# Plain product for the second block, rounding and block sums spread over turns, all score masks on VectorE

## The chip, the cores and the metric

The kernel runs on one core of a Trainium2 chip. The core has a matrix engine (TensorE, "PE" in the profile; its weight loads, "PEld", overlap the matmuls), a vector engine (VectorE, "DVE"), an activation engine (ScalarE, "ACT"), a general engine (GpSimd, "POOL") and a queue that issues most transfers (SyncE, "SP"). Each engine works off its own instructions in order; engines wait for each other through semaphores. The metric is the device time of one execution in microseconds: 628.98 us before the change, the median of three runs.

## The reference

Two parts follow each other: a gated linear attention (a state of 48 x 48 per head that decays and takes in one outer product per time step), and a feed-forward layer whose activation is h erf(softplus(h)).

```python
B, H, S, D = 4, 8, 768, 48
f = 1.0 / (1.0 + np.exp(-f_logit))
for t in range(S):
    state = f[:, :, t, :, None] * state + np.einsum('bhd,bhe->bhde', k[:, :, t], v[:, :, t])
    y[:, :, t] = np.einsum('bhd,bhde->bhe', q[:, :, t], state)
x = y.transpose(0, 2, 1, 3).reshape(3072, 384)
h = x @ w_in                                  # w_in 384 x 2048
sp = np.maximum(h, 0.0) + np.log1p(np.exp(-np.abs(h)))
out = (h * erf(sp)) @ w_out                   # w_out 2048 x 384
```

The two weights arrive with 64 bits a number.

## The kernel before

The 3072 tokens are 24 chunks of 128 and 12 blocks of two chunks. A chunk `g` passes four stages: `stage_d` (cumulated decays, decayed q and k), `stage_t` (transposes), `stage_s` (scores of the two half chunks, masked, and the new state) and `stage_y` (output, 128 tokens by 384). A block then gives 16 hidden tiles in four groups (`hidden`), each group is activated in ten steps (`activate`), and a projection makes the output rows.

An outer loop of 12 turns weaves all this together. One **slot** is one matmul of the hidden layer or the projection; the loop emits a slot and then, by counters, other work: a step of rounding, a stage of a chunk, a step of the activation, a step of sums. In turn `it`, the chunks of block it + 2 are worked on, the hidden tiles of block it + 1 are made, and block it - 2 is projected (from turn 2 on; turns 0 and 1 have hidden slots only).

```python
    def slots(it):

        if it == 0:
            h0, h1 = hiddens(0), hiddens(1)
            order = [h0[0], h0[1], h1[0], h0[2], h1[1], h0[3], h1[2], h1[3]]
            return chain(*order), 2 * n_h
        if it == 1:
            return chain(*hiddens(2)), n_h
        if it == 2:
            return chain(*hiddens(3), project_first(0)), n_h + n_ft * CPB
        if it < n_blocks - 1:
            return chain(project(it - 2), *hiddens(it + 1)), n_o + n_h
        return chain(*[project(blk) for blk in range(n_blocks - 3, n_blocks)]), 3 * n_o
```

**Masks.** The scores of a half chunk must keep only earlier time steps. Up to chunk 2 and from chunk 10 on VectorE multiplies them by a triangle straight from PSUM; for chunks 3 to 9 ScalarE copies and GpSimd masks:

```python
        for c in range(2):
            for r in range(2):
                if FIRST <= g < 2 * ADJACENT:

                    nc.scalar.copy(out=qA[half(1 - r), r, :, half(c)], in_=sc[half(c), r])
                    if c == 1:
                        flat = qA[half(1 - r), r].rearrange("s a (c t) -> s (a c) t", c=2)
                        nc.gpsimd.affine_select(
                            out=flat, in_=flat, pattern=[[0, 2 * HP], [1, C]], compare_op=ALU.is_ge,
                            fill=0.0, base=0, channel_multiplier=-1,
                        )
                    continue
                nc.vector.tensor_tensor(
                    out=qA[half(1 - r), r, :, half(c)], in0=sc[half(c), r],
                    in1=tri1[half(c)].unsqueeze(1).broadcast_to((C, HP, C)), op=ALU.mult,
                )
```

**Rounding.** Both weights come in 16 pieces of 768 KB (eight of `w_in`, then eight of `w_out`). `round_piece` turns one into 32 bits: one pass on ScalarE, then six on VectorE of 128 x 768 (lines 313 to 336). `weights_step` does about one of the six at a time, and the loop says how many per slot:

```python
            gen, n = slots(it)
            if it == 0:
                todo = [(stage_s, 2), (stage_y, 2), (stage_d, 3), (stage_t, 3), (stage_s, 3), (stage_y, 3),
                        (stage_d, 4), (stage_t, 4), (stage_d, 5), (stage_s, 4), (stage_t, 5),
                        (stage_y, 4)] + stages(2)[4:]
                at = [1, 5, 6, 12, 16, 23, 34, 42, 48, 52, 60, 74, 76, 80, 88, 94]
# ...
            for s, _ in enumerate(gen):
                due += (1 if s < 42 else 0.6 if s < 72 else 0.3) if it == 0 else 0.42 if it == 1 else 0.6
                while due >= 1:
                    weights_step()
                    due -= 1
```

**Projection.** Block 0 is projected plainly: 32 slots with 384 columns (`project_first`). The others use Winograd's form of Strassen's product: 7 products in place of 8, so 56 slots with 192 columns (`project`). It needs sums of blocks of the hidden (`sum_h`, four per group, on VectorE, once the group is activated), sums of blocks of `w_out` (`sum_w`, once, on GpSimd), and a combination of the products (L725).

```python
    def add(out, x, y, op=ALU.add, engine=nc.vector):
        engine.tensor_tensor(out=out, in0=x, in1=y, op=op)

    def sum_w(gi):
        w = w_out_sb[:, FG * gi : FG * (gi + 1), :]
        b11, b12 = w[:, 0:2, 0:DH], w[:, 0:2, DH:]
        b21, b22 = w[:, 2:4, 0:DH], w[:, 2:4, DH:]
        t = w_sums(gi)
        add(t[:, 0], b12, b11, ALU.subtract, nc.gpsimd)
        yield
        add(t[:, 1], b22, t[:, 0], ALU.subtract, nc.gpsimd)
        yield
        add(t[:, 2], b22, b12, ALU.subtract, nc.gpsimd)
        yield
        add(t[:, 3], b21, t[:, 1], ALU.subtract, nc.gpsimd)
# ...
    def sum_h(gr):

        while not gr["done"]:
            act_step()
        a11, a12, a21, a22 = blocks(gr["h"])
        sums = next(sum_places)
        add(sums[0], a21, a22)
        yield
        add(sums[1], sums[0], a11, ALU.subtract)
        yield
        add(sums[2], a12, sums[1], ALU.subtract)
        yield
        add(a21, a11, a21, ALU.subtract)
        gr["sums"] = sums
# ... in project_first, after the last slot of a group:
                    if j == FG - 1 and tt == CPB - 1:
                        to_sum.append(sum_w(gi))
# ... in project:
            for gi in gis:
                gr = groups[blk, gi]
                while gr["sums"] is None:
                    sum_step()
                        nc.tensor.matmul(
                            place[n], lhsT=x[:, j, :], rhs=y,
                            start=(gi == 0 and j == 0 and n in first),
                            stop=(gi == n_g - 1 and j == 1), skip_group_check=True,
                        )
                        yield
```

The sums of `w_out` are kept where the hidden of block 0 lay (`wT`), so each can be made only after block 0's product of that group.

**Activation steps and sum steps** in the loop:

```python
                if it < 2:
                    step = it == 1 and s % 6 == 3
                elif it == 2:
                    step = s % 5 in (1, 3)
                else:
                    step = s % 9 in (2, 6)
                if step:
                    act_step()
                if it == 2:
                    if s == n - 6:
                        to_sum.extend(sum_h(groups[1, gi]) for gi in range(NS))
                    sum_step()
                elif it > 2:
                    if s == n_o and it < n_blocks - 1:
                        to_sum.extend(sum_h(groups[it - 1, gi]) for gi in range(NS))
                    if it == n_blocks - 1 and s % n_o == 40 and s < 2 * n_o:
                        blk = n_blocks - 2 + s // n_o
                        to_sum.extend(sum_h(groups[blk, gi]) for gi in range(NS))
                    if s < n_o or s % 3 == 0 or it == n_blocks - 1:
                        sum_step()
```

```python
        h = gr["h"].rearrange("p j t -> p (j t)")
        e = epool.tile([P, FG * TB], FP32, name="e", tag="e")
        exp(e, h)
        yield
        n = len(SERF_KAB)
        xs = {}
        for i in range(n):
            xs[i] = xpool.tile([P, FG * TB], FP32, name="x", tag="x")
            other_set()
            term(xs[i], h, i)
            yield
        for i in range(n):
            times(e, xs[i], i)
            yield
        for _ in range(3):
            yield
        other_set()
        nc.scalar.activation(out=e[:], in_=e[:], func=AF.Tanh, scale=SERF_C)
        yield
        nc.vector.tensor_tensor(out=h, in0=h, in1=e[:], op=ALU.mult)
        gr["done"] = True
```

`act_step` moves each group that is being activated on by one step; a new group starts when the last has had five. `sum_h` calls `act_step` itself, as often as it takes, when its group is not activated yet.

Of the kernel before, what the change touches and what calls it, by code (L numbers as in the profile page):

```python
# [74 lines left out]
def kernel(  # L75
# [21 lines left out]
    CPB = 2  # L97
# [345 lines left out]
    def stage_s(g):  # L443
# [40 lines left out]
        for c in range(2):  # L484
            for r in range(2):
                if FIRST <= g < 2 * ADJACENT:

                    nc.scalar.copy(out=qA[half(1 - r), r, :, half(c)], in_=sc[half(c), r])  # L488
                    if c == 1:
                        flat = qA[half(1 - r), r].rearrange("s a (c t) -> s (a c) t", c=2)  # L490
                        nc.gpsimd.affine_select(
                            out=flat, in_=flat, pattern=[[0, 2 * HP], [1, C]], compare_op=ALU.is_ge,
                            fill=0.0, base=0, channel_multiplier=-1,
                        )
                    continue
# [105 lines left out]
    def places():  # L601
        own = [[sums_sb[:, b, n] for n in range(NA)] for b in range(NS)]
        for _ in range((n_blocks - 3) * n_g // NS):
# [4 lines left out]
        own = own[1::-1] + own[3:] + own[2:3]  # L608
# [5 lines left out]
    def add(out, x, y, op=ALU.add, engine=nc.vector):  # L614
        engine.tensor_tensor(out=out, in0=x, in1=y, op=op)  # L615

    def sum_w(gi):
# [4 lines left out]
        add(t[:, 0], b12, b11, ALU.subtract, nc.gpsimd)  # L622
        yield
        add(t[:, 1], b22, t[:, 0], ALU.subtract, nc.gpsimd)
        yield
        add(t[:, 2], b22, b12, ALU.subtract, nc.gpsimd)
        yield
        add(t[:, 3], b21, t[:, 1], ALU.subtract, nc.gpsimd)
# [30 lines left out]
    def project_first(blk):  # L659

        ops = ps_moe.tile([P, 2, 512], FP32, name="ops", tag="moe")
        for gi in range(n_g):
            gr = groups[blk, gi]
            for tt in range(CPB):
                for j in range(FG):
# [10 lines left out]
                    if j == FG - 1 and tt == CPB - 1:  # L676
                        to_sum.append(sum_w(gi))
# [82 lines left out]
    def slots(it):  # L760
# [7 lines left out]
        if it == 2:  # L768
            return chain(*hiddens(3), project_first(0)), n_h + n_ft * CPB
        if it < n_blocks - 1:  # L770
# [19 lines left out]
    with tc.manual_schedule():  # L790
# [8 lines left out]
        load(1, "qk")  # L799
        load_f(2)  # L800
        load_piece(0)
        load(1, "v")
        load(2)
        load_piece(1)
# [58 lines left out]
        stage_t(0)  # L863
        load(3, "qk")
# [327 lines left out]
```

## Time and profile before

| | before |
|---|---|
| time, median of 3 (lowest to highest) | 628.98 us (628.93 to 629.83) |
| span of the profiled execution | 627.6 us |
| TensorE busy | 589.5 us (94%), 5777 matmuls |
| VectorE busy | 470.2 us (75%), 788 instructions |
| ScalarE busy | 382.4 us (61%), 483 instructions |
| GpSimd busy | 38.4 us (6%), 49 instructions |
| mean granted TensorE clock | 0.974 |

Every matmul of 32-bit operands in the source is two matmul instructions in the trace. Busy time overlaps between the engines: it says how long an engine had work in hand, not that the work set the end. TensorE's mean durations overlap too (a matmul is in flight while the next starts), so the pace of a row of matmuls is read from the length of the row and not from the mean of one. The page's second part cuts the span into 40 slices of 15.7 us, a digit each (9 is 90% or more):

```profile
PE   8788699998976999999999999999999999999995
DVE  4998998695589778678787876797887694756751
ACT  5725457978864457756675776765775656556200
POOL 1000011010176000000000000000000000000000
PEclk9879799999989899999999999999999999999999
DMA  9997743440321043043052052052030000000000
```

The first six slices are full of transfers and of VectorE's work, GpSimd works mostly in slices 11 to 13, and from about the sixteenth slice on TensorE is full. A digit below 9 in the clock row is a slice in which TensorE ran slower for a part.

### The profile page before, as it was taken

To read this page: it belongs to the slowest core of one execution; us is meant where nothing else is said; L and a number is where in the kernel's file an instruction comes from. 1 tells how busy PE (TensorE), PEld (TensorE's weight loads), DVE (VectorE), ACT (ScalarE), POOL (GpSimd) and SP (SyncE) were. 2 spreads that over 40 slices of the span, in tenths; PEclk is the share of its full clock that TensorE was granted. 3 is DMA by queue.
4 is the path that set the end of the run, shared out by engine and by line. 5 is a ranking of instruction groups with operands and counts; after the bars stand their busy time and mean duration, and the time that the engine had idled before them with its cause. 6 is when DMAs were issued, how large, how long until landed. Compare 5 with 4: busy or idle time off the path is not lost.

```text
span 627.6 us, 13891 instructions
## 1 busy us (share of the span) xinstructions
PE 589.5 (94%) x5777; PEld 524.7 (84%) x5777; DVE 470.2 (75%) x788; ACT 382.4 (61%) x483; POOL 38.4 (6%) x49
## 2 busy tenths in 40 slices
PE   8788699998976999999999999999999999999995
PEld 7567588887644988988998998998998989989995
DVE  4998998695589778678787876797887694756751
ACT  5725457978864457756675776765775656556200
POOL 1000011010176000000000000000000000000000
PEclk9879799999989899999999999999999999999999
DMA  9997743440321043043052052052030000000000
GB/s 200 247 241 215 216 123 63 88 78 12 63 56 26 1 78 76 1 79 75 4 102 52 2 102 51 3 102 52 3 76 14 2 27 1 19 8 1 25 26 29
DMA packets 155587, 41.35 MB, mean 66 GB/s; under 512 B 147328, under 2 KB 150400, under 8 KB 155520
## 3 DMA queue, kind: packets, MB, share of 16 engines
q1 hardware_dynamic: 153440, 40.02, 29.3%
q8 instruction: 47, 0.77, 0.5%
q10 hardware_dynamic: 2080, 0.39, 0.3%
q14 instruction: 20, 0.16, 0.1%
HBM read 35.59 MB, written 4.72 MB: 64 GB/s over the span
## 4 chain that ended last, share of the span: by engine, by line
PE 72%; DVE 12%; issue 6%; ACT 5%; DMA 2%; SPq 1%; POOL 1%; DVEq 0%; ACTq 0%; POOLq 0%
PE ops L717 31%; PE hps L587 29%; PE y L525 3%; PE ps_t L411 2%; PE ops L670 2%; PE ps_d L380 2%; DVE sv L438 1%; PE sc L460 1%; PE sc L468 1%; DVE sv L439 1%; DVE w_in_sb L322 1%; DMA qn<-in_q_dram 1%; DVE qA L496 1%; DVE w_in_sb L336 1%; ACT L160 1%
## 5 line engine op out<-in xcount | busy, mean ns | idle before, releaser
L587 PE MATMUL hps<-xT,w_in_sb 128*128 128x256 f32 x1152 | 264.7, 386 | 7.8 <-DVE w_in_sb L336 4.4
L587 PEld LDWEIGHTS hps<-xT,w_in_sb 128*128 128x128 f32 x1152 | 218.2, 192 | 41.2 <-DVE w_in_sb L336 3.4
L165 DVE SCALAR_TENSOR_TENSOR e<-x,e 128x1024 f32<-128x1024 f32 x96 | 120.2, 1252 | 13.5 <-ACT x L160 13.2
L160 ACT ACTIVATE x<-Hg,serf_bias 128x1024 f32<-128x1024 f32 x88 | 97.6, 1141 | 0.2
L157 ACT ACTIVATE e<-Hg 128x1024 f32<-128x1024 f32 x44 | 46.6, 1058 | 77.0 <-DVE Hg L561 73.2
L717 PE MATMUL ops<-wT,Hg 128*128 128x192 f32 x352 | 87.6, 331 | 0.0
L717 PE MATMUL ops<-wT,scratch 128*128 128x192 f32 x320 | 76.5, 331 | 5.9 <-DVE scratch L615 5.9
L717 PE MATMUL ops<-w_out_sb,Hg 128*128 128x192 f32 x352 | 72.6, 329 | 0.0
L561 DVE TENSOR_TENSOR Hg<-Hg,e 128x1024 f32<-128x1024 f32 x44 | 54.6, 1240 | 22.5 <-ACT e L559 22.4
L717 PEld LDWEIGHTS ops<-wT,Hg 128*128 128x128 f32 x352 | 62.1, 192 | 2.2
L594 ACT COPY Hg<-hps 128x1024 f32<-128x1024 f32 x44 | 44.4, 1010 | 31.0 <-PE hps L587 30.7
L717 PEld LDWEIGHTS ops<-w_out_sb,Hg 128*128 128x128 f32 x352 | 60.7, 192 | 2.6
L717 PEld LDWEIGHTS ops<-wT,scratch 128*128 128x128 f32 x320 | 57.0, 193 | 6.2 <-issue 6.2
L559 ACT ACTIVATE e<-e 128x1024 f32<-128x1024 f32 x48 | 50.4, 1050 | 6.4 <-DVE e L165 6.3
L496 DVE TENSOR_TENSOR qA<-sc,tri 64x256 f32<-64x256 f32 x68 | 28.7, 422 | 22.3 <-PE sc L468 21.3
L725 DVE TENSOR_TENSOR scratch<-scratch,ops 128x384 f32<-128x384 f32 (+1 forms) x44 | 22.2, 504 | 30.3 <-ACT scratch L733 25.0
L418 ACT COPY qA<-ps_t 64x512 f32<-64x512 f32 x48 | 27.7, 578 | 22.5 <-PE ps_t L411 20.6
L395 DVE TENSOR_TENSOR qd<-qn,dp 128x384 f32<-128x384 f32 x24 | 13.4, 556 | 35.6 <-ACT dp L383 34.4
L717 PE MATMUL ops<-w_out_sb,scratch 128*128 128x192 f32 x160 | 39.5, 328 | 0.0
L525 PEld LDWEIGHTS y<-qA,sv 128*32 128x32 f32 x1536 | 24.6, 113 | 17.2 <-issue 9.2
L525 PE MATMUL y<-qA,sv 128*32 128x64 f32 x1536 | 28.9, 226 | 9.3 <-issue 6.9
L438 DVE TENSOR_TENSOR sv<-sc,sv 48x192 f32<-48x192 f32 x80 | 28.4, 354 | 8.3 <-ACT qA L488 6.9
(109 smaller groups left out, 648.9 us busy)
## 6 DMA issues: line engine op xcount, KB each, us to landing
lt<-in_f_logit_dram SPq DMA_DIRECT2D x24, 192.0 KB, 3.8
qn<-in_q_dram SPq DMA_DIRECT2D x24, 192.0 KB, 3.3
out_dram<-scratch SPq DMA_DIRECT2D x12, 384.0 KB, 2.6
kn<-in_k_dram SPq DMA_DIRECT2D x23, 192.0 KB, 3.5
vt<-in_v_dram SPq DMA_DIRECT2D x23, 192.0 KB, 3.6
sv<-in_v_dram SPq DMA_DIRECT2D x84, 48.0 KB, 2.9
w_out_sb<-in_moe_w_in_dram SPq DMA_DIRECT2D x4, 768.0 KB, 6.3
Hg<-in_moe_w_in_dram SPq DMA_DIRECT2D x4, 768.0 KB, 6.4
```

The lines of the kernel that those rows point to most:

```text
L157: nc.scalar.activation(out=dst[:], in_=h, func=AF.Exp)
L160: nc.scalar.activation(out=dst[:], in_=h, func=AF.Tanh, bias=serf_bias[:, i : i + 1], scale=SERF_KAB[i][0])
L165: nc.vector.scalar_tensor_tensor(out=e[:], in0=x[:], scalar=SERF_KAB[i][2], in1=e[:], op0=ALU.add, op1=ALU.mult)
L418: nc.scalar.copy(out=qAs[g][half(r), r], in_=pss[0][half(r)])
L438: nc.vector.tensor_tensor(out=new, in0=add, in1=old, op=ALU.add)
L496: nc.vector.tensor_tensor(out=qA[half(1 - r), r, :, half(c)], in0=sc[half(c), r], in1=tri1[half(c)].unsqueeze(1).broadcast_to((C, HP, C)), ...
L525: nc.tensor.matmul(y[M * i : M * (i + 1), kt, half(c)], lhsT=sv[:, r, c, a, o : o + M], rhs=qA[:, r, a, half(c)], start=(n == 0), stop=Tru ...
L559: nc.scalar.activation(out=e[:], in_=e[:], func=AF.Tanh, scale=SERF_C)
L561: nc.vector.tensor_tensor(out=h, in0=h, in1=e[:], op=ALU.mult)
L587: nc.tensor.matmul(hps[:, j, :], lhsT=w_in_sb[:, kt, ft * P : (ft + 1) * P], rhs=xTs[blk][:, kt, :], start=(kt == 0), stop=(kt == n_k - 1),)
L594: nc.scalar.copy(out=gr["h"], in_=hps[:])
L717: nc.tensor.matmul(place[n], lhsT=x[:, j, :], rhs=y, start=(gi == 0 and j == 0 and n in first), stop=(gi == n_g - 1 and j == 1), skip_grou ...
```

## The change

It alters five things together and leaves what is computed as it is.

- **Masks.** All chunks are masked on VectorE; the branch for chunks 3 to 9 goes.
- **Second block plain.** Block 1 is projected by `project_first` as block 0 is, at the start of turn 3, and needs no sums.
- **Block sums of w_out** are made by VectorE instead of GpSimd, on every second slot of turns 2 and 3.
- **Rounding** is spread: fewer steps per slot in turn 0, the last ones in turn 2.
- **Schedule.** Activation starts in turn 0 and its steps are spaced anew; the first two pieces of weights are loaded earlier and chunk 1's q and k later; the slots at which the stages of turns 0 and 3 are emitted move.

It is meant to even out VectorE's load and to take GpSimd and the early sums out of the way of the matmuls. The diff, with the plain renames and the list of places for the sums cut:

```diff
@@ stage_s
-                if FIRST <= g < 2 * ADJACENT:
-
-                    nc.scalar.copy(out=qA[half(1 - r), r, :, half(c)], in_=sc[half(c), r])
-                    if c == 1:
-                        flat = qA[half(1 - r), r].rearrange("s a (c t) -> s (a c) t", c=2)
-                        nc.gpsimd.affine_select(
-                            out=flat, in_=flat, pattern=[[0, 2 * HP], [1, C]], compare_op=ALU.is_ge,
-                            fill=0.0, base=0, channel_multiplier=-1,
-                        )
-                    continue
                 nc.vector.tensor_tensor(
@@ sum_w (and the same for the three others)
-        add(t[:, 0], b12, b11, ALU.subtract, nc.gpsimd)
+        add(t[:, 0], b12, b11, ALU.subtract)
@@ project_first
-                        to_sum.append(sum_w(gi))
+                        if blk == 0:
+                            to_sum.append(sum_w(gi))
@@ slots
+        if it == 3:
+            return chain(project_first(1), *hiddens(4)), n_ft * CPB + n_h
@@ the first loads
-        load(1, "qk")
+        load_piece(0)
+        load(1, "qkv")
+        load_piece(1)
         load_f(2)
-        load_piece(0)
-        load(1, "v")
         load(2)
-        load_piece(1)
         load_piece(2)
@@ before the first turn
         stage_t(0)
+        weights_steps(2)
         load(3, "qk")
@@ the turns
-                todo = [(stage_s, 2), (stage_y, 2), (stage_d, 3), (stage_t, 3), (stage_s, 3), (stage_y, 3),
+                todo = [(stage_s, 2), (stage_d, 3), (stage_y, 2), (stage_t, 3), (stage_s, 3), (stage_y, 3),
-                at = [1, 5, 6, 12, 16, 23, 34, 42, 48, 52, 60, 74, 76, 80, 88, 94]
+                at = [1, 5, 8, 12, 16, 23, 36, 43, 48, 52, 60, 74, 76, 80, 88, 94]
-                at = ([0] if it + 2 == ADJACENT else []) + [2, 26, 42, 54, 76, 90]
+                at = [0, 1, 15, 24, 31, 52, 66] if it + 2 == ADJACENT else [2, 26, 42, 54, 76, 90]
-                due += (1 if s < 42 else 0.6 if s < 72 else 0.3) if it == 0 else 0.42 if it == 1 else 0.6
+                due += (1 if s < 18 else 0.46 if s < 66 else 0.3) if it == 0 else 0.45
-                if it == 0 and s == 14:
+                if it == 0 and s == 24:
                     prepare(2, 0, CPB)
-                if it < 2:
-                    step = it == 1 and s % 6 == 3
-                elif it == 2:
-                    step = s % 5 in (1, 3)
+                if it == 0:
+                    step = s >= 24 and s % 8 == 5
+                elif it == 1:
+                    step = s % 5 == 3
+                elif it < 4:
+                    step = s % 7 in (1, 4)
+                elif it == n_blocks - 1:
+                    step = s % 3 == 1
                 else:
                     step = s % 9 in (2, 6)
                 if it == 2:
-                    if s == n - 6:
-                        to_sum.extend(sum_h(groups[1, gi]) for gi in range(NS))
-                    sum_step()
+                    if s % 2:
+                        sum_step()
                 elif it > 2:
-                    if s == n_o and it < n_blocks - 1:
+                    if s == n - n_h and it < n_blocks - 1:
                         to_sum.extend(sum_h(groups[it - 1, gi]) for gi in range(NS))
-                    if s < n_o or s % 3 == 0 or it == n_blocks - 1:
+                    if it == 3:
+                        if s % 2:
+                            sum_step()
+                    elif s < n_o or s % 3 == 0 or it == n_blocks - 1:
                         sum_step()
```

More of the change, by code (lines that the diff above doesn't have):

```diff
@@ L602, in places @@
         own = [[sums_sb[:, b, n] for n in range(NA)] for b in range(NS)]
-        for _ in range((n_blocks - 3) * n_g // NS):
+        for _ in range((n_blocks - 4) * n_g // NS):
             yield from own
@@ L607, in places @@
             own.insert(0, [x[:, 0 : S_WORDS // (NS * NA)].rearrange("p (j t) -> p j t", j=FG // 2) for x in t])
-        own = own[1::-1] + own[3:] + own[2:3]
+        own = own[1::-1] + own[2:]
         while True:
@@ L612, with add @@
     sum_places = places()
-    def add(out, x, y, op=ALU.add, engine=nc.vector):
-        engine.tensor_tensor(out=out, in0=x, in1=y, op=op)
+    def add(out, x, y, op=ALU.add):
+        nc.vector.tensor_tensor(out=out, in0=x, in1=y, op=op)
     def sum_w(gi):
@@ L621, in sum_w @@
         t = w_sums(gi)
-        add(t[:, 0], b12, b11, ALU.subtract, nc.gpsimd)
+        add(t[:, 0], b12, b11, ALU.subtract)
         yield
-        add(t[:, 1], b22, t[:, 0], ALU.subtract, nc.gpsimd)
+        add(t[:, 1], b22, t[:, 0], ALU.subtract)
         yield
-        add(t[:, 2], b22, b12, ALU.subtract, nc.gpsimd)
+        add(t[:, 2], b22, b12, ALU.subtract)
         yield
-        add(t[:, 3], b21, t[:, 1], ALU.subtract, nc.gpsimd)
+        add(t[:, 3], b21, t[:, 1], ALU.subtract)
     def blocks(h):
```

## The prediction

> **What bounds the kernel now.** I first read the page's busy shares (TensorE 94%, VectorE 75%, ScalarE 61%, GpSimd 6%), then the chain of work that ended last, and found where each turn of the outer loop begins by counting the matmuls of L587, L670 and L717 in TensorE's timeline. The windows of turns 0 to 3, with turn 5 as an undisturbed one, are this table (columns: TensorE, its weight loads, VectorE, ScalarE, GpSimd busy, then clock, DMA share and GB/s):
>
> ```profile
> 28.30:106.50 78.20, 67.99 (x739) 55.60 (x740) 72.72 (x120) 37.49 (x61) 5.80 (x8) 0.87 0.70 176
> 106.50:134.50 28.00, 27.59 (x368) 23.13 (x368) 20.61 (x36) 26.14 (x38) 3.15 (x4) 1.00 0.42 73
> 134.50:192.50 58.00, 52.12 (x440) 37.92 (x439) 41.59 (x49) 42.44 (x52) 19.60 (x16) 0.97 0.27 48
> 192.50:250.50 58.00, 51.03 (x535) 46.24 (x534) 47.79 (x80) 33.51 (x39) 6.81 (x7) 0.94 0.24 49
> 298.10:344.50 46.40, 46.40 (x487) 42.50 (x486) 36.93 (x65) 30.95 (x36) 0.00 (x0) 1.00 0.28 53
> ```
>
> From 298 us nearly to the end TensorE has no gap: the kernel is bound by matmuls there and only less matmul work could shorten it. What can be gained lies before. I work out the matmul time of a turn from undisturbed stretches of the chain: a hidden slot (two instructions) takes 20.72/96 x 2 = 0.432 us, a Winograd product slot 54.62/336 x 2 = 0.325 us, a plain projection slot (384 columns) twice that, 0.65 us, and one chunk of the attention (L380, L411, L460, L468, L525) 0.65 + 0.87 + 1.0 + 1.03 = 3.55 us. Turn 0 (96 hidden slots, 4 chunks) then needs 41.5 + 14.2 = 55.7 us and takes 78.2. Turn 1 (48, 2) needs 27.8 and takes 28. Turn 2 (48 hidden, 32 plain, 2 chunks) needs 20.7 + 20.8 + 7.1 = 48.6 and takes 58. Turn 3 (56 products, 48 hidden, 2 chunks and one extra score stage) needs 18.2 + 20.7 + 7.1 + 1.0 = 47 and takes 58. Turn 4 takes 47.6 against 46.4. That is 22.5 + 0.2 + 9.4 + 11 + 1.2 = 44 us above the matmul floor.
>
> What TensorE waited for there, by the list of waits over turns 0 to 3 (us in total, times, longest):
>
> ```profile
> PE ops L717 <- DVE scratch L615: 5.9, 1, 5.9
> PE ps_t L411 <- DVE qd L395: 5.6, 1, 5.6
> PE y L525 <- issue: 5.1, 3, 3.8
> PE hps L587 <- DVE w_in_sb L336: 4.4, 2, 3.0
> PE hps L587 <- DVE scratch L725: 1.1, 1, 1.1
> ```
>
> The first is the second block's Winograd sums at the opening of turn 3; the second and fourth are turn 0, where VectorE is 93% busy with rounding; the third ends at a y product in turn 2 (174 to 178 us) while GpSimd works off masks and block sums in its queue. Two waits cost again in clock: the table shows 0.87 in turn 0, and in turn 3 the matmuls after 203 us run at half rate for about 5 us.
>
> A third view, VectorE's own timeline, shows what the average hides: its operations double in length while GpSimd works.
>
> ```profile
> 187.54 1.23 DVE L615 TENSOR_TENSOR scratch<-Hg 128x256 f32<-128x256 f32 x1
> 188.69 2.03 DVE L165 SCALAR_TENSOR_TENSOR e<-x,e 128x1024 f32<-128x1024 f32 x1
> ...
> 206.09 1.22 DVE L165 SCALAR_TENSOR_TENSOR e<-x,e 128x1024 f32<-128x1024 f32 x1
> ...
> 209.49 0.42 DVE L615 TENSOR_TENSOR scratch<-Hg 128x256 f32<-128x256 f32 x1
> ```
>
> The same two operations take 2.03 and 1.23 us beside GpSimd's sums and 1.22 and 0.42 us after them. Adding the excess of all VectorE operations from 172 to 199 us gives about 9.8 us.
>
> **What the Trainium skill says.** "SBUF — State Buffer", section "Who interferes with whom": a VectorE instruction with two SBUF inputs contends with a GpSimd instruction that reads SBUF, and the one that comes second waits for the whole of the other. The lines above agree: an excess of 0.8 us each, no longer than one GpSimd sum. "GPSIMD Engine Reference", section "4.1 Engine selection": two-input elementwise work belongs on VectorE, GpSimd being about 2 times slower; here 128x384 takes GpSimd 1.4 to 1.5 us (L615, contention included) and VectorE 0.556 us (L395). "TensorE: Matmul & The Clock Gate", section "What's actually happening": an idle window of some 3.4 us halves the clock; the 5.9 us wait followed by half-rate matmuls agrees.
>
> **The change, part by part.**
>
> Plain second block: 56 product slots (18.2 us) become 32 plain slots (20.8 us), so turn 3 needs 2.6 us more of TensorE: 49.6 us. In return its four groups need no sums (16 x 0.44 = 7.0 us of VectorE) and no combination (L725, 4 x 0.5 = 2 us), and the 5.9 us wait loses its reason: the plain product asks only for finished activations, 45 activation steps at its fourth group, and the new schedule has done 9 + 9 + 23 + 7 = 48 there.
>
> Block sums of w_out on VectorE: 16 x 0.556 = 8.9 us more there, spread over turns 2 and 3, against 9.8 us of contention gone. About nothing on VectorE, and GpSimd's queue drops out of the path to y.
>
> Masks on VectorE: chunks 3 to 9, 4 x 0.422 = 1.7 us each, 11.8 us in all (three chunks in turn 0, two in turn 1, two in turn 2). ScalarE loses 28 copies of 0.367 us.
>
> Rounding spread: a step costs (0.556 + 0.56 + 0.96 + 0.56 + 0.965 + 0.96)/6 = 0.76 us of VectorE and there are 96. Steps before the first slot go from 10 to 12, in turn 0 from 67 to 49, in turn 1 from 19 to 22, in turn 2 from none to 13.
>
> Activations earlier: 9 steps in turn 0 (none before), 9 in turn 1 (8), 23 in turn 2 (32). Five steps carry one group, with three VectorE operations of 1.22 us.
>
> VectorE's need by turn:
> - Turn 0: 72.7 - 18 x 0.76 + 12 x 0.422 + 3 x 1.22 - about 1 of contention = 66.7 us against 55.7 of TensorE.
> - Turn 1: 20.6 + 1.1 + 3.4 + 3.7 = 28.8 against 27.8.
> - Turn 2: 41.6 - 7.5 contention - 1.3 sums of the hidden + 3.4 masks + 12 x 0.556 + 13 x 0.76 - 6.7 activations = 46 against 48.6.
> - Turn 3: 47.8 - 3.2 contention - 5.7 sums - 2 combination + 2.2 block sums = 39 against 49.6.
>
> So VectorE stays the bound in turn 0, ties in turn 1 and nearly in turn 2, and is free in turn 3. In turn 5 it is 80% busy without a gap on TensorE; above some 93% I expect short waits, since each mask and each decayed query stands in one queue with rounding and activations. I choose 71 us for turn 0 (66.7 plus some 4 of waits; it had 5.5 idle before), 31 for turn 1, 52 for turn 2, 51 for turn 3, 46.6 for turn 4. Against 78.2, 28, 58, 58 and 47.6 this is -7 + 3 - 6 - 7 - 1 = **-18 us**. The start before the first hidden matmul (28.3 us) I leave unchanged: the first piece is loaded earlier and rounded two steps earlier, but chunk 1's q and k land one 768 KB transfer later, and both are needed. The last eight turns keep their matmuls. 628.98 - 18 = **611 us**.
>
> **Rivals.** (1) VectorE becomes the bound through turn 2. The masks, the late rounding and the block sums all go to the engine that was already the bound in turn 0; if every y waits for its mask, turns 0 to 2 take 74, 34 and 55 us and turn 3 53: -4 + 6 - 3 - 5 - 1 = -7, 622 us. For it: the tie in turn 1. Against it: turn 1 had 7.4 us of VectorE idle, mostly waiting for a full ScalarE queue (26.1 of 28 us) that now gets lighter. (2) The waits go wholly, TensorE being able to run a few us ahead of VectorE, and the clock stays up: 67, 29, 50 and 50 us, -11 + 1 - 8 - 8 - 1 = -27, 602 us. (3) The early load order costs: if chunk 1's late q and k hold up the first xT by the 3.3 us that a piece takes at 240 GB/s, 614 us. (4) The 2.6 us of extra matmuls outweigh all, the old waits merely moving into activations: 632 us. The forced activation steps were the reason for the 5.9 us, and the count above leaves three spare, so I give this little.
>
> **Range and chances.** Between rivals (2) and (1), with more weight near the middle: 603 to 621 in 8 of 10. 2% faster is 616.4; half the span between 611 and rival (1) is beyond it, and rival (3) lies below it. Faster by over 2%: 0.72; within 2%: 0.25; slower by over 2%: 0.03.
>
> **What would show it.** No VectorE operation of L165 near 2 us between 170 and 200 us, and GpSimd idle after the start but for memsets. L670 with twice the instructions (x128), at the 0.325 us interval. The 5.9 us wait of L717 on L615 gone. Turn 3 near 51 us with VectorE below 42 us busy. Turn 0 shorter by some 7 us with VectorE still above 90%. Wrong would be: turn 0 as long as before (then the loads or the chunk chain bound it, not rounding), y products in turns 1 and 2 waiting for the masks of L496 by several us, a low clock in turns 1 and 2, or a first hidden matmul later than 30 us.

## The result, and the profile after

The changed kernel takes **625.44 us** (625.18 to 625.52), the kernel before 629.17 us beside it: a ratio of 0.9938, interval 0.9921 to 0.9956. Foreseen were 611 us. Two rows of the page show that the parts work as meant, though: GpSimd is idle (4.2 us), and VectorE's long operation is back at its short time.

```profile
POOL 1000000000000000000000000000000000000000
...
L165 DVE SCALAR_TENSOR_TENSOR e<-x,e 128x1024 f32<-128x1024 f32 x96 | 117.2, 1220 | 13.7 <-ACT x L160 13.2
...
L486 DVE TENSOR_TENSOR qA<-sc,tri 64x256 f32<-64x256 f32 x96 | 40.5, 422 | 30.4 <-PE sc L468 28.8
```

L165 has a mean of 1220 ns with no 2 us cases left; the masks (L486) are 96, 28 more than before. The windows of turns 0 to 4 answer to those of the prediction (window and its length, then TensorE, weight loads, VectorE, ScalarE, GpSimd busy, clock, DMA share, GB/s):

```profile
29.70:102.00 72.30, 62.59 (x736) 50.26 (x736) 65.02 (x115) 41.22 (x56) 0.92 (x2) 0.98 0.72 187
102.00:136.00 34.00, 30.04 (x374) 24.16 (x373) 28.86 (x50) 23.70 (x31) 0.00 (x0) 1.00 0.37 64
136.00:195.50 59.50, 51.95 (x439) 37.71 (x438) 51.53 (x79) 33.69 (x39) 0.00 (x0) 0.94 0.26 45
195.50:245.50 50.00, 50.00 (x486) 37.19 (x485) 37.91 (x64) 37.04 (x42) 0.51 (x2) 1.00 0.27 54
245.50:292.10 46.60, 46.60 (x487) 42.70 (x486) 37.52 (x66) 30.71 (x36) 0.00 (x0) 1.00 0.27 51
```

Turn 3 is 50.0 us with TensorE never idle, as foreseen. But turn 1 takes 34 us where it took 28, and turn 2 takes 59.5 with VectorE 51.5 us busy. Turn 3 therefore opens at 195.5 us, later than the 192.5 us of before: what turn 0 gained was lost again at the start and in turns 1 and 2. The list of TensorE's waits over turns 0 to 3 (us in total, times, longest) has one that stands out:

```profile
PE hps L577 <- ACT Hg L584: 6.4, 1, 6.4
PE y L515 <- DVE sv L439: 4.6, 7, 1.0
PE hps L577 <- DVE w_in_sb L336: 3.8, 3, 1.4
```

It is found in the three timelines around 157 us (start, duration, engine, line; in brackets the idle time before, and what ended it). ScalarE first:

```profile
152.62 1.28 ACT L347 ACT_TABLE_LOAD   x1
160.67 0.84 ACT L364 ACTIVATE lt<-lt 128x768 f32<-128x768 f32 x1 [6.76 <-DVE lt L360]
161.54 0.84 ACT L365 ACTIVATE lt<-lt 128x768 f32<-128x768 f32 x1
162.41 1.01 ACT L584 COPY Hg<-hps 128x1024 f32<-128x1024 f32 x1
```

After its table load ScalarE waits 6.76 us for one VectorE instruction, the clamp L360 of the next block's logits. Behind the clamp's exp and log stands the copy of a hidden group out of PSUM (L584). TensorE needs that copy's buffer:

```profile
153.79 3.29 PE L577 MATMUL hps<-xT,w_in_sb 128*128 128x256 f32 x14
163.47 1.22 PE L577 MATMUL hps<-xT,w_in_sb 128*128 128x256 f32 x2 [6.39 <-ACT Hg L584]
164.49 1.49 PE L380 MATMUL ps_d<-lt,tri 128*128 128x384 f32 x2
165.77 4.66 PE L577 MATMUL hps<-xT,w_in_sb 128*128 128x256 f32 x16
```

It stands idle 6.39 us. The next matmuls also run slower: 16 hidden instructions take 4.66 us, against 3.72 in the row that starts at 143.0 us. The row of VectorE says why the clamp was late:

```profile
154.66 0.55 DVE L313 TENSOR_SCALAR w_out_sb<-w_out_sb 128x768 f32<-128x768 f32 x1
155.12 1.22 DVE L165 SCALAR_TENSOR_TENSOR e<-x,e 128x1024 f32<-128x1024 f32 x1
...
157.88 0.69 DVE L422 COPY kT<-ps_t 128x512 f32<-128x512 f32 x1
158.61 0.56 DVE L317 TENSOR_SCALAR w_out_sb<-w_out_sb 128x768 uint32<-128x768 uint32 x1
159.20 0.96 DVE L322 SCALAR_TENSOR_TENSOR w_out_sb<-scratch,w_out_sb 128x768 uint32<-128x768 uint32 x1
160.08 0.56 DVE L360 TENSOR_SCALAR lt<-lt 128x768 f32<-128x768 f32 x1
...
169.55 0.56 DVE L395 TENSOR_TENSOR qd<-qn,dp 128x384 f32<-128x384 f32 x1 [4.19 <-ACT dp L383]
```

VectorE isn't waiting for anything up to the clamp. It is working through rounding (L313, L317, L322), the activation (L165) and a copy (L422), one after the other, and starts the clamp at 160.1 us, 6.2 us after ScalarE's table load had ended. Then it is VectorE's turn to idle, 4.19 us, for ScalarE's decay factors (dp), which the stopped queues had delayed.

### The profile page after: what moved, and what is told of

It reads as the page before. It is cut to its first block, busy times and chain, and to the rows that moved or that the text cites. A ratio compares the mean times of both kernels' runs of the same rounds, so it can differ in the third digit from the quotient of the medians.

```text
span 623.7 us, 13720 instructions
## 1 busy us (share of the span) xinstructions
PE 587.6 (94%) x5729; PEld 512.8 (82%) x5729; DVE 470.3 (75%) x812; ACT 374.4 (60%) x457; POOL 4.2 (1%) x19
## 3 DMA queue, kind: packets, MB, share of 16 engines
q1 hardware_dynamic: 153440, 40.02, 29.2%
## 4 chain that ended last, share of the span: by engine, by line
PE 72%; DVE 16%; ACT 4%; issue 2%; DMA 2%; SPq 2%; DVEq 0%; ACTq 0%
PE hps L577 31%; PE ops L708 25%; PE ops L660 7%; PE y L515 3%; PE ps_t L411 2%; DVE qA L486 2%; PE ps_d L380 2%; DVE sv L438 1%; DVE sv L439 1%; PE sc L468 1%; PE sc L460 1%; DVE e L165 1%; ACT x L160 1%; DMA lt<-in_f_logit_dram 1%; DVE w_in_sb L322 1%
## 5 line engine op out<-in xcount | busy, mean ns | idle before, releaser
L165 DVE SCALAR_TENSOR_TENSOR e<-x,e 128x1024 f32<-128x1024 f32 x96 | 117.2, 1220 | 13.7 <-ACT x L160 13.2
L157 ACT ACTIVATE e<-Hg 128x1024 f32<-128x1024 f32 x44 | 46.6, 1058 | 69.4 <-DVE Hg L551 65.2
L708 PE MATMUL ops<-wT,Hg 128*128 128x192 f32 x320 | 78.9, 328 | 0.0
L708 PE MATMUL ops<-wT,scratch 128*128 128x192 f32 x288 | 67.8, 326 | 0.9 <-DVE scratch L716 0.9
L584 ACT COPY Hg<-hps 128x1024 f32<-128x1024 f32 x44 | 44.4, 1009 | 37.0 <-PE hps L577 36.7
L708 PE MATMUL ops<-w_out_sb,Hg 128*128 128x192 f32 x320 | 65.1, 326 | 0.0
L486 DVE TENSOR_TENSOR qA<-sc,tri 64x256 f32<-64x256 f32 x96 | 40.5, 422 | 30.4 <-PE sc L468 28.8
L708 PEld LDWEIGHTS ops<-wT,Hg 128*128 128x128 f32 x320 | 55.8, 190 | 1.9
L708 PEld LDWEIGHTS ops<-w_out_sb,Hg 128*128 128x128 f32 x320 | 54.6, 190 | 2.0
L708 PEld LDWEIGHTS ops<-wT,scratch 128*128 128x128 f32 x288 | 50.2, 190 | 1.1 <-issue 1.1
L395 DVE TENSOR_TENSOR qd<-qn,dp 128x384 f32<-128x384 f32 x24 | 13.4, 557 | 37.5 <-ACT dp L383 37.4
L515 PE MATMUL y<-qA,sv 128*32 128x64 f32 x1536 | 29.3, 221 | 10.0 <-DVE sv L439 4.9
L418 ACT COPY qA<-ps_t 64x512 f32<-64x512 f32 x48 | 27.7, 577 | 15.5 <-PE ps_t L411 15.1
L708 PE MATMUL ops<-w_out_sb,scratch 128*128 128x192 f32 x144 | 35.2, 326 | 0.0
L439 DVE TENSOR_TENSOR sv<-sv,Tall 48x192 f32<-48x192 f32 x80 | 28.2, 353 | 2.8
```

The source lines that it names most:

```text
L157: nc.scalar.activation(out=dst[:], in_=h, func=AF.Exp)
L165: nc.vector.scalar_tensor_tensor(out=e[:], in0=x[:], scalar=SERF_KAB[i][2], in1=e[:], op0=ALU.add, op1=ALU.mult)
L439: nc.vector.tensor_tensor(out=new, in0=new, in1=total, op=ALU.mult)
L486: nc.vector.tensor_tensor(out=qA[half(1 - r), r, :, half(c)], in0=sc[half(c), r], in1=tri1[half(c)].unsqueeze(1).broadcast_to((C, HP, C)), ...
L515: nc.tensor.matmul(y[M * i : M * (i + 1), kt, half(c)], lhsT=sv[:, r, c, a, o : o + M], rhs=qA[:, r, a, half(c)], start=(n == 0), stop=Tru ...
L584: nc.scalar.copy(out=gr["h"], in_=hps[:])
```

## The experiments

All times are medians beside runs of the kernel before on the same chip. "Opens" is the start of the first projection matmul of a turn in the trace, so the columns cut each time into its stretches.

| run | time, us | ratio to before (interval) | first hidden | turn 3 opens | turn 4 opens | turn 11 opens | span |
|---|---|---|---|---|---|---|---|
| before | 629.17 | | 28.3 | 192.5 | 250.3 | 566.4 | 627.6 |
| after | 625.44 | 0.9938 (0.9921 to 0.9956) | 29.7 | 195.5 | 245.5 | 561.6 | 623.7 |
| e1 clamp early | 618.66 | 0.9827 (0.9802 to 0.9852) | 30.0 | 188.4 | 238.3 | 554.6 | 616.7 |
| e2 round early | 625.29 | 0.9942 (0.9922 to 0.9963) | 29.5 | 195.3 | 245.3 | 561.4 | 623.3 |
| e3 masks back | 620.14 | 0.9855 (0.9832 to 0.9877) | 29.7 | 190.4 | 240.3 | 556.4 | 618.7 |
| e4 plain alone | 626.94 | 0.9966 (0.9952 to 0.9980) | 27.5 | 192.8 | 246.7 | 562.8 | 625.7 |
| e5 sums on GpSimd | 626.86 | 0.9964 (0.9950 to 0.9978) | 31.3 | 196.5 | 246.4 | 562.5 | 625.5 |
| e6 old loads | 627.48 | 0.9979 (0.9970 to 0.9989) | 27.5 | 196.9 | 246.9 | 563.0 | 625.2 |
| e7 rounding left out | 606.77 | 0.9649 (0.9633 to 0.9666) | 30.9 | 177.0 | 227.0 | 543.6 | 605.9 |
| e8 clamp early, masks back | 615.87 | 0.9793 (0.9776 to 0.9810) | 30.0 | 186.0 | 235.9 | 552.2 | 614.5 |
| e9 all but the plain block | 630.96 | 1.0036 (1.0025 to 1.0048) | 29.2 | 194.0 | 245.0 | 561.1 | 625.6 |
| e13 the same, a second profile | 630.63 | one run | 29.5 | 195.9 | 246.9 | 563.0 | 628.8 |
| e10 all clamps early | 618.06 | 0.9830 (0.9812 to 0.9849) | 29.8 | 187.9 | 237.9 | 554.1 | 616.1 |
| e11 clamps early, masks by turn | **614.31** | 0.9775 (0.9753 to 0.9797) | 29.3 | 184.1 | 234.1 | 550.4 | 612.3 |
| e12 before, clamp early | 628.88 | 1.0002 (0.9992 to 1.0012) | 27.4 | 195.2 | 251.4 | 567.6 | 628.4 |
| e14 clamps early, rounding early | 619.51 | 0.9860 (0.9836 to 0.9883) | 29.7 | 189.5 | 239.5 | 555.8 | 617.9 |

My theory after the result (A) was that one small instruction late in VectorE's queue had stopped two other engines. The rival (B) was that VectorE's whole work up to the end of turn 2 sets the time, wherever it blocks; the weaker rival (C), that ScalarE itself is full.

**e1: the clamp alone, earlier.**

```diff
-                if it + 3 < n_blocks and s == prepare_at:
-                    prepare(it + 3, 0, CPB)
+                if 1 <= it and it + 3 < n_blocks and s == max(0, prepare_at - 16):
+                    clamp(it + 3, 0, CPB)          # the VectorE instruction L360
+                if it + 3 < n_blocks and s == prepare_at:
+                    prepare(it + 3, 0, CPB, clamped=it >= 1)
```

(`clamp` is split off `prepare`; the clamps of turns 1 to 8 move, those of turn 0 stay)

> The changed kernel with one reordering: from turn 1 on, VectorE's clamp of a block's logits (L360, 0.56 us) is emitted 16 slots (about 7 us) ahead of ScalarE's exp and log that need it, not directly before them. No work is added or removed. Theory A (one clamp late in VectorE's queue holds ScalarE's queue, behind it the hidden copy, behind that TensorE): the 6.4 us wait of the hidden matmuls on ScalarE's copy at 157 us and some 2 us of half-rate matmuls after it go, 625.4 - 8 = about 617 us. Theory B (VectorE's total work through turn 2 sets the time, wherever the queue blocks): the wait moves to the next mask or decayed query, 623 to 625 us. Theory C (ScalarE itself is full there): no change, 625 us.

618.66 us, 6.8 less, with the same instructions. Turn by turn, from 0 to 2:

```profile
29.90:102.70 72.80, 63.21 (x735) 50.85 (x736) 64.85 (x115) 41.14 (x56) 0.92 (x2) 0.95 0.74 188
102.70:135.50 32.80, 31.14 (x373) 25.40 (x372) 30.30 (x51) 23.85 (x31) 0.00 (x0) 0.95 0.40 69
135.50:188.30 52.80, 49.95 (x438) 36.22 (x437) 48.76 (x77) 33.66 (x39) 0.00 (x0) 1.00 0.28 50
```

Turn 2 falls from 59.5 to 52.8 us, at full clock. ScalarE passes the same place without a pause:

```profile
150.59 1.28 ACT L347 ACT_TABLE_LOAD   x1
151.88 0.85 ACT L369 ACTIVATE lt<-lt 128x768 f32<-128x768 f32 x1
152.76 0.84 ACT L370 ACTIVATE lt<-lt 128x768 f32<-128x768 f32 x1
153.63 1.01 ACT L589 COPY Hg<-hps 128x1024 f32<-128x1024 f32 x1
```

So A holds for turn 2, and C falls: ScalarE's work is the same. What A doesn't explain is that turns 0 and 1 stay at 73 and 33 us.

**e2: rounding back in turn 0.**

```diff
-                due += (1 if s < 18 else 0.46 if s < 66 else 0.3) if it == 0 else 0.45
+                due += (1 if s < 42 else 0.6 if s < 72 else 0.3) if it == 0 else 0.42 if it == 1 else 0.6
```

> The changed kernel with the rounding counters of before (1 step a slot to slot 42, then 0.6 and 0.3 in turn 0; 0.42 in turn 1): the rounding moves from turns 1 and 2 back to turn 0. Theory A: turn 0 some 5 us longer, turn 2 loses the 6.4 us wait and the slow clock because VectorE is not behind there, turn 1 about 2 us shorter: 619 to 621 us. Theory B: VectorE has the same work up to the end of turn 2, so 624 to 626 us.

625.29 us, unchanged, and turn 3 opens at the same 195.3 us. The wait of turn 2 is gone (turn 2 is 49.7 us there, TensorE full), but turn 0 has grown to 82.8 us, with waits of its own over the same list:

```profile
PE ps_t L411 <- DVE qd L395: 5.6, 2, 4.0
...
PE ps_d L380 <- ACT lt L365: 4.6, 3, 2.9
```

The decayed query (L395) and the clamp's log (L365) are now late in turns 0 and 1. B's number, and a warning: the same work put elsewhere found another small instruction to hold up.

**e3: masks of chunks 3 to 9 back on ScalarE and GpSimd** (the removed branch put back in `stage_s`).

> The changed kernel with the masks of chunks 3 to 9 back on ScalarE (copies) and GpSimd, nothing else altered. Theory A and B alike: VectorE has 11.8 us less to do through turn 2 (some 2 us come back as contention), its queue is shorter, the late clamp comes earlier and the 6.4 us wait shrinks or goes: 616 to 621 us, which would say that the masks on VectorE were the part of the change that cost. Theory C: ScalarE gets 10 us of copies more and delays the hidden copies further: 627 us or more.

620.14 us, 5.3 less than the change: of the parts taken back one by one (e2, e3, e5, e6, e9) the masks are the only one that had cost. Two of TensorE's waits over turns 0 to 3:

```profile
PE y L525 <- issue: 6.7, 5, 2.9
PE hps L587 <- ACT Hg L594: 2.8, 1, 2.8
```

The wait for the hidden copy is down to 2.8 us, but y waits 6.7 us in five places ("issue" here is time that the profile ascribes to nothing). It isn't GpSimd that y waits for. The longest of the five ends 0.10 us after ScalarE's copy of the transposed query (L418):

```profile
150.21 1.17 ACT L418 COPY qA<-ps_t 64x512 f32<-64x512 f32 x2
151.48 1.27 PE L525 MATMUL y<-qA,sv 128*32 128x64 f32 x64 [2.92 <-issue]
```

GpSimd had done its masks by 147.8 us. ScalarE had four mask copies (1.5 us) to do before, from 144.8 us; in the changed kernel, without them, the same y waited 1.15 us for the same copy. The four other waits, too, end about 0.1 us after an instruction of ScalarE (L418) or VectorE (L439).

**e4: the plain second block alone, in the kernel before.**

```diff
+        if it == 3:
+            return chain(project_first(1), *hiddens(4)), n_ft * CPB + n_h
-                    if s == n - 6:
-                        to_sum.extend(sum_h(groups[1, gi]) for gi in range(NS))
+                elif it == 3:
+                    step = s % 7 in (1, 4)
```

(with turn 3's places, and no sums of w_out from block 1)

> The kernel before with one part of the change alone: block 1 projected plainly in turn 3, with the places of turn 3's stages and its activation steps (2 in 7 slots) that go with it. Masks, rounding, block sums, loads and turns 0 to 2 stay as before. If the gain of turn 3 (58 to 50 us in the changed kernel) comes from the plain product alone: 629.2 - 8 = 621 us, better than the whole change. If it needs the activations spread over turns 0 to 2 or GpSimd free of block sums: turn 3 stays at 54 or more and the time at 625 to 629 us.

626.94 us. Turn 3 took 54.0 us: shorter than 57.8, longer than the 50.0 in the changed kernel. The missing 4 us are a 2.0 us wait of the hidden matmuls on ScalarE's copy at 230 us, behind activation steps that the sums of block 2 called for, and a lower clock after it (0.90 to the end of the turn).

**e5: w_out's sums back on GpSimd.**

```diff
-        add(t[:, 0], b12, b11, ALU.subtract)
+        add(t[:, 0], b12, b11, ALU.subtract, nc.gpsimd)   # and the three others
```

> The changed kernel with w_out's block sums back on GpSimd, all else as changed. If contention costs VectorE about what the sums themselves do (the prediction's 9.8 against 8.9 us): 624 to 627 us, with VectorE's 128x1024 operations near 2.0 us again while the sums run. If the move of the sums to VectorE had been what filled its queue in turn 2: 619 us or less. If GpSimd's slower sums hold up the second half of turn 2 or the first products of turn 4: over 628 us.

626.86 us, 1.4 more than the change; the contention is back in VectorE's timeline, operations of 128x1024 beside GpSimd's sums and between them:

```profile
182.52 2.02 DVE L551 TENSOR_TENSOR wT<-wT,e 128x1024 f32<-128x1024 f32 x1
184.46 2.03 DVE L165 SCALAR_TENSOR_TENSOR e<-x,e 128x1024 f32<-128x1024 f32 x1
187.20 1.24 DVE L165 SCALAR_TENSOR_TENSOR e<-x,e 128x1024 f32<-128x1024 f32 x1 [0.71 <-ACT x L160]
```

Turns 2 and 3 of this run:

```profile
137.00:196.50 59.50, 51.95 (x438) 37.71 (x437) 48.48 (x66) 33.71 (x39) 17.63 (x13) 0.94 0.25 45
196.50:246.40 49.90, 49.90 (x485) 37.11 (x484) 36.47 (x61) 36.97 (x42) 4.07 (x6) 1.00 0.27 55
```

VectorE has 16 operations less than in the changed kernel, 8.9 us of work, but its busy time falls by 4.5 us only: the contention gives 4.4 us back, half of what it cost in the kernel before. So the sums on VectorE do cost it 4.5 us. They cost the kernel nothing: both turns are as long as in the changed kernel, and the 6.4 us wait is there in both. What the run lost lies where no sum is made: the first hidden matmul comes 1.6 us later, and the last turn is 0.9 us longer. That the move gained anything is not shown.

**e6: the first loads and rounding steps as before.**

```diff
-        load_piece(0)
-        load(1, "qkv")
-        load_piece(1)
-        load_f(2)
+        load(1, "qk")
+        load_f(2)
+        load_piece(0)
+        load(1, "v")
```

(and `load_piece(1)` after chunk 2; without the two early steps)

> The changed kernel with the order of the first loads and the first rounding steps of before. If the early first piece delays chunk 1 (first hidden matmul at 29.7 us after the change, 28.3 before): first hidden matmul near 28.3 us, and 1 us less in all, 624 us. If the two early rounding steps relieve turn 0: turn 0 gets 1.5 us longer and the time stays at 625 to 626 us.

627.48 us, 2.0 more. The first hidden matmul does come earlier, 27.5 us, but the matmuls then wait for rounded weights:

```profile
PE hps L577 <- DVE w_in_sb L336: 10.8, 4, 5.0
```

10.8 us against 3.8. The earlier pieces and rounding steps together are worth about 2 us although they delay the start by as much; I had foreseen a gain, or no change.

**e7: rounding left out** (clamp early; five of the six VectorE passes of each piece dropped, so that the weights are only a rough copy and the output isn't the reference's).

```diff
-        nc.vector.tensor_scalar(out=halves(bits), ..., scalar1=0x07FFFFFF, scalar2=3, ...)
         yield
-        nc.vector.scalar_tensor_tensor(out=bits, ...)
         yield                                  # and three more
```

> The kernel with the early clamp, and five of the six VectorE passes of each rounding piece left out (only the first, the lower bound, stays, so the weights are wrong); loads and ScalarE's pass stay. It takes 16 x 4.0 = 64 us of VectorE's work out of turns 0 to 2. Theory B for what is left (VectorE's work is the bound of turns 0 and 1): turn 0 falls from 73 to about 57 us, turn 1 from 33 to 28.5, turn 2 from 53 to 49: 618.7 - 16 - 4.5 - 4 = 594 us. If the arrival of the weights (transfers at 0.7 of the engines in turn 0) or the chain of the chunks bounds turn 0: it stays above 66 us and the time above 604 us.

606.77 us, 11.9 below e1, and not the 594 us of theory B. Turns 0 to 2:

```profile
30.90:97.00 66.10, 60.10 (x735) 49.88 (x736) 31.41 (x70) 41.11 (x56) 0.51 (x2) 0.97 0.77 199
97.00:127.50 30.50, 29.31 (x373) 24.11 (x372) 18.66 (x35) 23.83 (x31) 0.00 (x0) 1.00 0.41 71
127.50:177.00 49.50, 49.50 (x440) 36.42 (x439) 36.73 (x61) 33.65 (x39) 0.00 (x0) 1.00 0.30 55
```

Turns 1 and 2 fall to 30.5 and 49.5 us, near the matmuls' own 27.8 and 48.6: there the bound was VectorE. Turn 0 stops at 66 us, 10 above its matmuls' need, with VectorE idle for more than half of it. VectorE waits once for a transfer:

```profile
75.55 0.35 DVE L428 TENSOR_TENSOR sv<-sv,Tall 48x192 f32<-48x192 f32 x1 [8.24 <-DMA Tall<-dp]
```

The decay factors of a chunk (Tall) travel in eight copies of 0.5 KB, and SyncE's queue, which issues them one after the other, also issues the pieces of w_out and the chunks' loads:

```profile
67.42 7.79 SPq L380 DMA_DIRECT2D Tall<-dp  x8
```

ScalarE had the factors ready at 63.9 us; loads went first until 67.4 us, and the eight copies took until 75.2 us to issue. Behind the stalled VectorE stood turn 0's clamp, which stays in its place in e7: ScalarE waited 9.31 us for it, and TensorE's own largest wait follows:

```profile
PE ps_d L369 <- ACT lt L354: 5.0, 1, 5.0
```

So under the rounding of turn 0 a second limit lies hidden, small transfers in a busy queue, and it takes over when the first is removed. It reached TensorE once more by way of a clamp; how much of the 10 us an early clamp in turn 0 would have saved, no run shows.

**e8: clamp early and masks back.** The edits of e1 and e3 together.

> The early clamp and the masks of chunks 3 to 9 back on ScalarE and GpSimd together. If both act on the same wait (the late clamp of turn 2): no more than the better of the two alone, 617 to 619 us. If the masks cost VectorE's time in their own right (theory B, 10 us less to do through turn 2, turns 0 and 1 bound by it): 613 to 615 us.

615.87 us, 2.8 below e1 (2.1 by the two ratios), between the two ranges foreseen. The masks therefore cost in their own right and not only by the late clamp. By turns: turns 0 and 1 take 70.9 and 31.1 us, 3.6 us less together than in e1, and turn 2 takes 54.0, 1.2 us more.

**e9 and e13: all of the change but the plain block.**

```diff
-        if it == 3:
-            return chain(project_first(1), *hiddens(4)), n_ft * CPB + n_h
+                    if s == n - 6:
+                        to_sum.extend(sum_h(groups[1, gi]) for gi in range(NS))
```

(with before's places of turn 3's stages, of the sums, and its activation steps in turn 3)

> The changed kernel without one part: block 1 keeps Winograd's products and its sums (asked for in the last six slots of turn 2, as before), with before's places for turn 3's stages and steps; masks, rounding, block sums and loads as changed. If the plain block is the part that made turn 3 short (58 to 50 us): turn 3 is near 58 us again and the time about 633 us, so that the change without it is slower than no change. If moving GpSimd's work away already makes turn 3 short: turn 3 about 51 us and 625 to 627 us.

> The run without the plain block once more, for a second profile: the first profile (627.3 us) lay 3.6 us below that kernel's median of 630.96 us, so it doesn't show where the median's time goes. If turn 3 carries it: turn 3 at 54 to 58 us and a time near 631 us. If turns 0 to 2 carry it: turn 3 again at 51 us and the opening of turn 3 at 197 us or later, not 194.

630.96 us, 5.5 more than the change. Yet turn 3 is 51.0 us in both profiles, so the 5.9 us wait on the block sums had shrunk to 1.1 us without the plain block. What is lost lies elsewhere. The second profile opens turn 4 at 246.9 us, 1.4 us later than the changed kernel; turns 4 to 10 take 316.1 us in both; and the last turn, from its opening to the end of the span, takes 65.8 us (62.1 after). The list of waits of that last turn has one entry, over turn 11 of the second profile:

```profile
PE ops L708 <- DVE scratch L716: 3.2, 1, 3.2
```

A product there waits 3.2 us for the combination of an earlier block (0.9 us in the changed kernel). The first profile's span is 3.2 us shorter: it opens turn 3 1.9 us earlier, and its last turn is 1.3 us shorter. The last turn has the same wait of 3.2 us in both; in the 6 us after it the granted clock was 1.00 in the first and 0.76 in the second. Why that product waits longer without the plain block stays open.

**e10: all clamps early**, turn 0 too.

> As the run with the early clamp, and in turn 0 too the two clamps are emitted 16 slots ahead. ScalarE waited 10 us for clamps in turns 0 and 1 there. If those waits reach TensorE (theory A in turn 0): 1 to 3 us less, 616 to 617 us. If turn 0 is bound by VectorE's work or by the loads: 618 to 619 us.

618.06 us, not clear of e1's 618.66. ScalarE's 10 us of waits for clamps were down to 1.9; they had not been on the path.

**e11: clamps early, masks where the engine has room.**

```diff
+                if FIRST <= g < 8:
+                    nc.scalar.copy(...)            # and GpSimd's affine_select, as before
```

> All clamps early, and the masks of chunks 3 to 7 (turns 0 and 1) on ScalarE and GpSimd, those of chunks 8 and 9 (turn 2) on VectorE. With all masks back turns 0 and 1 were 3.3 us shorter and turn 2 was 1 us longer, with 2.9 us waits of y behind GpSimd. If the best place of a mask goes by the engine that is full in its turn: 614 to 615 us, 1 to 2 us below the run with all masks back. If not: 616 us or more.

**614.31 us**, the fastest version here that leaves no work out, 1.6% below the changed kernel by the two ratios (0.9775/0.9938). It is within the range foreseen, but not for the reason foreseen. Its turns 0 to 2 take 69.4, 31.1 and 54.2 us, those of e8 70.9, 31.1 and 54.0. Turn 2 gained nothing from having its masks on VectorE: the waits of y put down to "issue" fell from 6.7 to 1.3 us, but others came, up to 1.7 us on ScalarE's copy of a hidden group. What e11 gains over e8 lies at the start and in turn 0, where it also has the clamps early. So masks off VectorE are worth it in turns 0 and 1; which engine is best for them in turn 2 is not shown.

**e12: the early clamp in the kernel before.**

> The kernel before with the early clamp alone (from turn 1 on). VectorE is not behind in turn 2 there (ScalarE waited less than 0.1 us for that clamp) so theory A expects no gain from it: 628 to 629.5 us. If the early clamp is worth something by itself, whatever the change: 623 us or less.

628.88 us, no change. The kernel before didn't need it, as VectorE was not late there; ScalarE goes on from its table load without an idle time:

```profile
153.84 1.28 ACT L347 ACT_TABLE_LOAD   x1
155.13 0.84 ACT L369 ACTIVATE lt<-lt 128x768 f32<-128x768 f32 x1
```

**e14: all clamps early, rounding early.**

> All clamps early, with the rounding counters of before (rounding back in turn 0). If, once the clamp blocks nothing, VectorE's work up to the end of turn 2 alone sets the opening of turn 3 (theory B), then where the rounding lies does not matter: 617 to 619 us as with all clamps early. If spreading the rounding is worth something by itself, because late rounding lies beside matmuls that turn 0 lacks: 621 to 625 us.

619.51 us against 618.06 of e10, just outside the 617 to 619 us foreseen, and turn 3 opens 1.6 us later. So with the clamps out of the way the place of the rounding matters little (TensorE still has a wait of 6.9 us on the decayed query in turn 0): VectorE has 145.3 us of work between the first hidden matmul and turn 3 in e14, 143.7 in e10, in stretches of 159.8 and 158.1 us. Against e2, which has the rounding in the same places, e14 is 5.8 us shorter: turns 0 to 2 take 159.8 us for 165.8, and the 4.6 us of waits on the clamp's log are gone. With the rounding early it was the clamps of turns 0 and 1 that cost.

## Why the prediction was wrong, step by step

- **VectorE's need by turn** was right but in one place: foreseen 66.7, 28.8, 46 and 39 us, measured 65.0, 28.9, 51.5 and 37.9. Turn 2 is 5.5 us over. Its rounding took 15.5 us; before the change it took 2.6 us there, and the sum had added 9.9. I had counted where work is emitted; an engine that runs late does it a turn later. That is 3 of the 5.5 us; most of the rest is the activation, 15 long operations of 1.22 us where the sum left between 13 and 14.
- **The step that failed** is the term for VectorE's waits, "above some 93% I expect short waits". The 71, 31 and 52 us chosen for turns 0 to 2 allow 12.5 us of them over VectorE's need. They were 20.4 us (165.8 of length, 145.4 busy). Turn 0 (72.3 for 71) and turn 3 (50.0 for 51) hold, turn 1 is 3 over, turn 2 is 7.5 over. In turn 2 one wait of TensorE is 6.4 us, with a lower clock after it. e1 shows it: without the late clamp turn 2 is 52.8 us and the whole 618.66, within the range that I had given; VectorE's waits are 14.5 us there. The argument took a late instruction to cost its own lateness once. This one was what the head of another engine's queue waited for, with TensorE's buffer behind it. Turn 1's 3 us go with VectorE's load: it takes 31.1 us with the masks away (e8), 30.5 with the rounding away (e7).
- **Of the signs of being wrong** that I had named, one came: a low clock in turn 2 (0.94). y waited 1.4 us in all for masks, not several each.
- **Rival (1)**, VectorE as the bound through turn 2, was the nearest: 622 us foreseen. It had turn 0 at 74 and turn 1 at 34 (72.3 and 34.0), turn 2 at 55 (59.5). Its road, every y waiting for its mask, was not the one taken. e3, e8 and e14 say that VectorE's work holds as a floor below the clamp: taking 12 us of masks away from VectorE gains 2.8 us with the clamp early and 5.3 with it late. e7 says that it is not the whole floor of turn 0.
- **The plain block** was not what made turn 3 short, nor needed to remove the 5.9 us wait: from 57.8 us, turn 3 falls to 54.0 with the block alone (e4), to 51.0 with all the rest (e9), to 50.0 with both. In e9 the block sums are made with GpSimd idle and with activations done earlier; which of the two shrank the wait, no run separates. In the whole change the block saves 1 us in turn 3 and, by e9 and e13, 2.4 to 3.7 us in the last turn, on which the prediction had nothing.
- **The sums of w_out** cost the kernel nothing, as foreseen, but not because work and contention cancel: 8.9 us of work stand against 4.4 us of contention in the new schedule (e5), and the wait on the clamp hides the difference.
- **GpSimd in the path to y** is not what the trace shows. The y product that waited until 178.2 us in the kernel before started just after a copy on VectorE had ended (L422, at 178.1 us); GpSimd's masks were done at 172.1. GpSimd's part was to stretch VectorE's operations before that copy (L439 took 1.29 us in place of 0.35).
- **The start**, left unchanged, came 1.4 us later, and what it buys in turn 0 (e6) was not in the sum.
- **What the later turns give back** was taken as nothing. A 1.2 us loss that turn 4 had before lies in turn 6 now (47.6 us for 46.4), and the last turn is 0.9 us longer.

By stretches: the start costs 1.4, turn 0 is 5.0 shorter, turn 1 4.6 longer, turn 2 1.9 longer, turn 3 7.8 shorter, turn 4 1.2 shorter, the rest 2.1 longer (turns bounded by the exact count of matmuls, which puts 0.7 us of turn 0's old window into turn 1). The sum is the spans' difference, 627.6 to 623.7, within rounding.

## What to carry to other kernels

Adding up an engine's work per stage tells whether it fits, not what its lateness will stop: before giving an in-order engine more work, list the short instructions in its queue that the head of another engine's queue will wait for, and emit those early. Emitting the clamps of 0.56 us 16 slots earlier was worth more (6.8 us) than the whole change (3.7 us), and nothing in the kernel before (e12), where VectorE was not late. And where work can go to several engines, the choice is one per stage: the masks off VectorE shortened turns 0 and 1 by 3.6 us and lengthened turn 2 by 1.2 (e8). A gain foreseen for the best mix has still to be read turn by turn: e11 got its gain in another turn than foreseen.

## What the runs showed of the hardware

Small copies cost time in the queue that issues them: in e7 SyncE took 7.79 us to issue eight copies of 0.5 KB, one after the other, and VectorE waited 8.24 us for them (median from issue to landing in the kernel before: 2.1 us). In the changed kernel the same eight were issued from 68.7 to 76.1 us, and VectorE, still at its rounding, came to them at 79.6 us without a wait.

After an idle time of 6.39 us TensorE ran its next matmuls at a lower clock: turn 2's mean was 0.94, and 1.00 in e1 without that wait. Near 3 us it went either way. In e3 a wait of 2.92 us was followed by 14 hidden instructions in 3.29 us, and one of 2.85 us, some 7 us later, by 16 in 5.30. The same 3.2 us wait of the last turn cost 1.3 us more in e13 than in e9. So these waits cost up to some 2 us more than their length, and two executions of one kernel can differ in that.
